# Stage 6 of a fused attention and expert kernel: second layer in three products of split operands

## The chip, the cores and the metric

The kernel runs on one core of a Trainium2 chip. Its engines have queues of their own: PE (TensorE, matmuls), DVE (VectorE), ACT (ScalarE), POOL (GpSimd) and SP (SyncE, which here issues DMAs). The metric is the time of one execution on the device in microseconds, lower is better.

## The reference

Three layers in a row over 1152 tokens (2 batches of 576), all in float32. The first is attention in which every query keeps its 32 largest scores; the second is a mixture of four experts, in which stage 6, the subject here, lies; the third is a feed-forward layer with the maximum of three products. In short:

```python
scores = scale * np.matmul(q, k.transpose(0, 1, 3, 2))
kth = np.partition(scores, -top_k, axis=-1)[..., -top_k:-top_k + 1]
attn = softmax(np.where(scores >= kth, scores, -1e9))     # 8 heads of 64
x = (attn @ v) as 1152 x 512
for e in range(4):                                         # _moe_ref
    h = np.maximum(x @ w1[e], 0.0)                         # 512 -> 1024
    out += p[:, e:e + 1] * (h @ w2[e])                     # 1024 -> 512
h = np.maximum(np.maximum(x @ w1, x @ w2), x @ w3)         # _moe2_ref, 512 -> 768
return h @ w_out
```

## The kernel before

The tokens are 9 tiles of 128. Attention goes tile by tile and pair of heads by pair of heads; its top-32 search (L443, L445) fills DVE for the first 440 us. PE has room meanwhile, and the kernel puts the experts' matmuls between those of attention. The experts run in stages that each take one, two or three tiles: `STAGES` is [0], [0,1], [1,2], [2,3], [3,4], [4,5], [5], [6,7,8], [6,7,8], counted from 0. A stage takes some of eight pieces `i` of the hidden layer: piece i is half of expert i // 2, and its two halves are u = 0, 1, 256 hidden units each. Stage 6 takes tile 5 alone (the sixth tile) with i = 0 to 3. Every (i, u) has a weight unit `a` of the first layer and one `b` of the second, 128x1024 each, keyed `(c, "a" or "b", i, u)` with c the stage.

**Two ways to multiply.** Most matmuls are done in three products (`product`, L680 to L682): each operand is split into a rounded high part (fp32r) and the low part that is left, and high x low, high x high and low x high are added up in PSUM. For a weight this takes a load to `raw` (L212), a copy by ACT to `whi` (L271) and a subtraction to `wlo` (L277), by POOL in two halves of 128x512 or, from a certain unit on (`LATE`), by DVE in one piece for every second unit. The hidden layer gets its high part from ACT with the relu and its low part from DVE (L822, L824); every `ON_POOL_H`-th time ACT writes `raw` (L815) and copies it (L816), and POOL subtracts (L817). The other way is a plain fp32 matmul of whole operands, slower per column but without splits. Stages in `WHOLE` (0 and 6) use it: in stage 6 `whole()` loads both `a` and `b` units straight into the buffers that hi and lo parts use elsewhere (L262 to L267), L801 does the first layer, ACT the relu (L804, `hfull`), and L842 the second layer, four matmuls of 128x512 for each i. A matmul in fp32 leaves two records in the trace, one in fp32r one.

**What sets the order.** One Python program writes out all instructions; engines then run their own queues strictly in that order. Attention's steps come first. Between them a planner adds expert work: `clock["dve"]` adds up a price for DVE work (`dve(n)`), `clock["goal"]` rises with it, and expert steps are put in until the priced PE work (`pe(n)`) reaches the goal. `later(...)` holds an evacuation back by one or two steps. `w_split_to` writes a weight's load and split `W_AHEAD` = 4 units before its use. There are five buffers each for raw, high and low parts. While the last stages of the experts run, the weights of the third layer, which come in a wide format, are converted in 48 pieces (`to_float32`: ACT L238 and L239, DVE L241 to L245, POOL L248 and a DMA on ACT's queue at L253); the first starts when attention is over. At about 582 us the first turned tiles (L900 transposes, ACT L906 and DVE L907 split) open the third layer.

**Names.** A tile's name carries a number that counts allocations, so the same tile has different numbers before and after. h_5640 is the last hidden block of stage 5, with its low part made by POOL; whi, wlo and raw are as above; psr (L517) are the transposed reciprocals of attention's row sums, ps1 and ps2 the sums of first and second layer, acc the gated sum of a tile (L743).

Of the kernel before, what the change touches and what calls it, by code (L numbers as in the profile page):

```python
# [10 lines left out]
F32 = mybir.dt.float32  # L11
# [3 lines left out]
AF = mybir.ActivationFunctionType  # L15
ALU = mybir.AluOpType
# [44 lines left out]
def kernel(  # L61
# [14 lines left out]
    nc = tc.nc  # L76
    B, HP, D, _, S = k.shape
    NT, DM = out.shape
    E = gates.shape[2]
    P = 128  # L80
# [20 lines left out]
    STAGES = [[0]] + [[t - 1, t] for t in range(1, NTILE - 3)] + [[NTILE - 4]] + [[NTILE - 3, NTILE - 2, NTILE - 1]] * 2  # L101
# [28 lines left out]
    def dve(n):  # L130
        clock["dve"] += 0.07 + n / 960.0

    def pe(n):
        clock["pe"] += n / 2400.0
# [63 lines left out]
    w_pos = {"load": 0, "split": 0}  # L198

    def whole(key):  # L200
        return key[1] in "ab" and key[0] in WHOLE

    def w_load_to(n):
        while w_pos["load"] < min(n, len(order)):
# [78 lines left out]
    def weight(key, oldest=None):  # L283

        w_split_to(w_index[oldest or key] + W_AHEAD + 2 * whole(key))
        return w_hl[key]
# [385 lines left out]
    def later(*stages):  # L672
        tick()
        lag.append(list(stages))
# [114 lines left out]
    def experts():  # L789
        begin = {}  # L790

        def half1(c, i, u):
            tiles = STAGES[c]
            N = len(tiles) * P
            if c in WHOLE:
                ps = bank("ps1")
                w = weight((c, "a", i, u)).rearrange("p (a f) -> p a f", f=256)
                for f in range(2):
                    for a in range(KT):
                        pe(4 * P)  # L800
                        nc.tensor.matmul(ps[:, f * P:(f + 1) * P], lhsT=w[:, a, f * P:(f + 1) * P], rhs=xfull[:, a, :], start=f == a == 0, stop=f == 1 and a == KT - 1)  # L801
                    yield True
                h = hp_.tile([P, 2, 512], F32, tag="h", bufs=4, name="hfull")[:, 0, 0:2 * P]
                later(lambda: [nc.scalar.activation(out=h, in_=ps[:, 0:2 * P], func=AF.Relu), made.add(("h", c, i, u))])  # L804
                yield h
                return
            for groups in layer1(weight((c, "a", i, u)), xs_of(tiles), N, begin.pop((c, i, u), None)):
                if groups is None:
                    tick()
                    yield True  # L810
            hh, hl = hidden(N)
            count = made_h[0] = made_h[0] + 1
            if ON_POOL_H and not count % ON_POOL_H:
                raw = ms.tile([P, 2 * WIDTH], F32, tag="tm", bufs=2, name="raw")
                later(lambda: [nc.scalar.activation(out=raw[:, g], in_=ps, func=AF.Relu) for g, ps in groups],  # L815
                      lambda: [nc.scalar.activation(out=hh[:, 0:2 * N], in_=raw[:, 0:2 * N], func=AF.Copy),  # L816
                               nc.gpsimd.tensor_tensor(out=hl[:, 0:2 * N], in0=raw[:, 0:2 * N], in1=hh[:, 0:2 * N].bitcast(F32), op=ALU.subtract),  # L817
                               made.add(("h", c, i, u))])
                yield hh, hl
                return  # L820
            dve(2 * N)
            later(lambda: [nc.scalar.activation(out=hh[:, g], in_=ps, func=AF.Relu) for g, ps in groups],  # L822
                  *[lambda: None] * H_LAG,
                  lambda: [nc.vector.scalar_tensor_tensor(out=hl[:, g], in0=ps, scalar=0.0, in1=hh[:, g].bitcast(F32),  # L824
                                                          op0=ALU.max, op1=ALU.subtract) for g, ps in groups]
                  + [made.add(("h", c, i, u))])
            yield hh, hl

        outs = {}

        def half2(c, i, hs, ti):
            t = STAGES[c][ti]
            if not i % 2:
                outs[t] = po.tile([P, DM], F32, tag="o", name="ps2") if ti < 2 else bank("ps2")
            ps = outs[t]
            assert {("h", c, i, 0), ("h", c, i, 1)} <= made
            if c in WHOLE:
                for u in range(2):
                    w = weight((c, "b", i, u), (c, "b", i, 0)).rearrange("p (f n) -> p f n", f=2)
                    for f in range(2):  # L840
                        pe(4 * DM)
                        nc.tensor.matmul(ps, lhsT=hs[u][:, f * P:(f + 1) * P], rhs=w[:, f, :], start=not i % 2 and u == f == 0, stop=i % 2 == 1 and u == f == 1)  # L842
                        yield True
            else:
                yield from layer2(ps, [weight((c, "b", i, u), (c, "b", i, 0)) for u in range(2)], hs, len(STAGES[c]) * P, ti, not i % 2, i % 2 == 1)
            if not i % 2:
                return
            first = t not in accs
            if first:
                sums(t)  # L850
            later(*[lambda: None] * E_LAG, gated(ps, t, i // 2, first, c == LAST_IN[t] and i == HALVES[c][-1]))

        before = None
        for c in range(1, len(STAGES)):
            phase[0] = c
            newest = max(STAGES[c])
            if c == 1:
                i = HALVES[c][0]
                for parts in (range(HP - 2), (HP - 2,)):
                    while (newest, parts[-1]) not in x_ready:  # L860
                        yield None
                    for n, x in enumerate([(i, 0), (i, 1), (i + 1, 0), (i + 1, 1)]):
                        if not parts[0]:
                            begin[(c, *x)] = (po if n < 2 else pg).tile([P, 512], F32, tag="go"[n < 2], name="ps1")
                        yield from begun(begin[(c, *x)], weight((c, "a", *x), (c, "a", i, 0)), xs_of(STAGES[c]), 2 * P, parts)
                        flush()
            while (newest, HP - 1) not in x_ready:
                yield None
            for i in HALVES[c]:
                hs = []  # L870
                for u in range(2):
                    for y in half1(c, i, u):
                        if y is not True:
                            hs.append(y)
                        yield True
                if i == HALVES[c][-1]:
                    x_free.update(t for t in STAGES[c] if LAST_IN[t] == c)
                if before is not None:
                    for ti in range(len(STAGES[before[0]])):
                        yield from half2(*before, ti)  # L880
                before = c, i, hs
        flush()
        yield from turned_ahead(len(STAGES))
        for ti in range(len(STAGES[before[0]])):
            yield from half2(*before, ti)
        flush()
# [193 lines left out]
```

## Time and profile before

| what | value |
|---|---|
| median of three runs | 749.8 us (749.56 to 750.65) |
| profiled execution, its own time | 748.98 us |
| its span on the core | 747.1 us |
| PE busy | 724.6 us, 97% |
| DVE, ACT, POOL busy | 605.4, 493.6, 459.4 us |
| granted PE clock | 1.0 over the whole span |
| L842 in stage 6 | 32 records of 0.592 us, from 429.9 to 465.1 us |

The span runs from the first to the last instruction; the rest of the execution's time lies around it. A row of the timeline begins with the start and the length in us; PE's rows overlap by the depth of its pipeline, so work is best read from the start of one group to the start of the next. An arrow in square brackets gives the idle time ahead of an instruction and what ended it.

### The profile page before, as it was taken

The page shows a single profiled execution, that of the slowest core. Times are in us where ns is not written, and L with a number is a line of the kernel's source. Part 1 is how long each engine was busy: PE and PEld are TensorE (multiplying, and loading weights), DVE is VectorE, ACT ScalarE, POOL GpSimd, SP SyncE. Part 2 cuts the span into 40 slices and gives each one's busy share as a digit, 9 for nine tenths or more (in the row PEclk, how much of TensorE's full clock was granted, in tenths as well). Part 3 has the DMA queues.
Part 4 walks back from the last instruction along what each step waited for, and adds up shares of the span by engine and source line. Part 5 has one row for each costly group of instructions (what it writes and reads, how often), then busy time and mean ns, then how long its engine had stood idle before and what let it go on. Part 6 is the DMA issues. An engine that isn't in the chain of part 4 may idle for free.

```text
span 747.1 us, 13552 instructions
## 1 busy us (share of the span) xinstructions
PE 724.6 (97%) x4678; PEld 641.4 (86%) x4678; DVE 605.4 (81%) x1160; ACT 493.6 (66%) x1127; POOL 459.4 (61%) x400
## 2 busy tenths in 40 slices
PE   6799999999999999999999999999999999999998
PEld 3587689888989989898988967999988899999996
DVE  6999989989999899999999958999999644233341
ACT  4668889899977787798796665666455533442531
POOL 2514778679979797698775216677676733442520
PEclk9999999999999999999999999999999999999999
DMA  7584555545647353545442859788788452443501
GB/s 220 180 269 160 147 174 175 156 127 159 194 123 209 108 195 122 154 126 162 144 121 91 288 182 363 240 268 278 231 259 255 157 191 76 154 170 99 196 2 43
DMA packets 56484, 130.14 MB, mean 174 GB/s; under 512 B 9760, under 2 KB 23328, under 8 KB 56416
## 3 DMA queue, kind: packets, MB, share of 16 engines
q1 hardware_dynamic: 48064, 120.69, 51.9%
q10 hardware_dynamic: 8352, 8.59, 3.2%
q8 instruction: 37, 0.61, 0.3%
q14 instruction: 31, 0.25, 0.1%
HBM read 120.60 MB, written 8.65 MB: 173 GB/s over the span
## 4 chain that ended last, share of the span: by engine, by line
PE 68%; DVE 13%; ACT 9%; POOL 4%; issue 3%; DMA 2%; ACTq 0%; POOLq 0%
PE ps L680 16%; PE ps L682 16%; PE ps L681 16%; DVE m L443 6%; DVE work L445 5%; POOL wlo L277 4%; PE psv L534 3%; ACT whi L271 3%; PE pss L423 2%; PE psp L489 2%; PE ps L842 2%; PE pso L680 2%; PE psa L765 2%; PE pso L681 2%; PE pso L682 2%
## 5 line engine op out<-in xcount | busy, mean ns | idle before, releaser
L277 POOL TENSOR_TENSOR wlo<-raw,whi 128x512 fp32r<-128x512 f32 x228 | 303.4, 1361 | 108.3 <-ACT whi L271 106.6
L271 ACT ACTIVATE whi<-raw 128x1024 fp32r<-128x1024 f32 x148 | 152.6, 1056 | 34.1 <-POOL narrow L248 14.6
L680 PE MATMUL ps<-xl,whi 128*128 128x256 f32 (+1 forms) x520 | 159.6, 307 | 0.6 <-POOL xl L555 0.6
L682 PE MATMUL ps<-xh,wlo 128*128 128x256 f32 (+1 forms) x520 | 156.5, 301 | 0.0
L681 PE MATMUL ps<-xh,whi 128*128 128x256 f32 (+1 forms) x520 | 156.4, 301 | 0.0
L443 DVE MAX8 m<-work 128x8 f32<-128x576 f32 x216 | 155.0, 743 | 0.1
L445 DVE MATCH_REPLACE8 work<-m,work 128x576 f32<-128x576 f32 x144 | 106.5, 740 | 0.0
L680 PEld LDWEIGHTS ps<-xl,whi 128*128 128x128 f32 x520 | 98.5, 189 | 1.9 <-POOL xl L555 0.8
L277 DVE TENSOR_TENSOR wlo<-raw,whi 128x1024 fp32r<-128x1024 f32 x34 | 53.5, 1573 | 56.4 <-ACT whi L271 45.2
L681 PEld LDWEIGHTS ps<-xh,whi 128*128 128x128 f32 x520 | 97.7, 188 | 1.2 <-issue 0.7
L682 PEld LDWEIGHTS ps<-xh,wlo 128*128 128x128 f32 x520 | 97.6, 188 | 0.0
L248 POOL TENSOR_TENSOR narrow<-narrow,raw 128x256 int32<-128x256 int32 x48 | 45.4, 947 | 40.0 <-DVE narrow L245 13.4
L680 PE MATMUL ps<-wlo,h 128*128 128x512 f32 x160 | 65.5, 410 | 0.6 <-POOL wlo L277 0.6
L682 PE MATMUL ps<-whi,h 128*128 128x512 f32 x160 | 62.8, 393 | 1.3 <-POOL h L817 1.3
L681 PE MATMUL ps<-whi,h 128*128 128x512 f32 x160 | 62.8, 392 | 0.0
L430 ACT ACTIVATE s<-pss 128x288 f32<-128x288 f32 x144 | 51.4, 401 | 11.8 <-PE pss L418 11.3
L443 DVE MAX8 m<-s 128x8 f32<-128x576 f32 x72 | 53.8, 747 | 3.9 <-ACT s L430 3.9
L445 DVE MATCH_REPLACE8 work<-m,s 128x576 f32<-128x576 f32 x72 | 53.3, 740 | 0.0
L682 PE MATMUL ps<-x2h,wlo 128*128 128x384 f32 x144 | 48.5, 336 | 0.0
L681 PE MATMUL ps<-x2h,whi 128*128 128x384 f32 x144 | 48.3, 335 | 0.0
L680 PE MATMUL ps<-x2l,whi 128*128 128x384 f32 x144 | 48.2, 335 | 0.0
L947 DVE TENSOR_TENSOR tm<-ps,tm 128x384 f32<-128x384 f32 x36 | 19.8, 554 | 33.6 <-PE ps L682 31.8
(118 smaller groups left out, 1616.2 us busy)
## 6 DMA issues: line engine op xcount, KB each, us to landing
raw<-in_w_dram SPq DMA_DIRECT2D x112, 512.0 KB, 4.2
raw<-narrow SPq DMA_DIRECT2D x36, 512.0 KB, 3.9
whole<-in_w_dram SPq DMA_DIRECT2D x30, 512.0 KB, 5.4
raw<-in_m_dram SPq DMA_DIRECT2D x36, 256.0 KB, 4.6
narrow<-narrow ACTq DMA_DIRECT2D x48, 128.0 KB, 4.7
kraw<-in_k_dram SPq DMA_DIRECT2D x16, 288.0 KB, 4.5
qraw<-in_q_dram SPq DMA_DIRECT2D x48, 64.0 KB, 3.9
raw<-in_mo_dram SPq DMA_DIRECT2D x12, 256.0 KB, 3.8
```

The costliest lines, as they stand in the source:

```text
L248: nc.gpsimd.tensor_tensor(out=out.bitcast(I32), in0=out.bitcast(I32), in1=last, op=ALU.add)
L271: nc.scalar.activation(out=hi, in_=raw, func=AF.Copy)
L277: on.tensor_tensor(out=lo[:, x], in0=raw[:, x], in1=hi[:, x].bitcast(F32), op=ALU.subtract)
L423: nc.tensor.matmul(ps[:, 0:SH], lhsT=l, rhs=r, start=i == 0, stop=i == len(mm) - 1)
L430: nc.scalar.activation(out=s[:, h, :], in_=halves[h][:, 0:SH], func=AF.Copy)
L443: nc.vector.max(m[:, 8 * r:8 * r + 8], src)
L445: nc.vector.match_replace(out=self.w[j], in_to_replace=m[:, 8 * r:8 * r + 8], in_values=src, imm_value=NEG)
L534: nc.tensor.matmul(ps[j * D:(j + 1) * D, cols], lhsT=vs[:, j * NR + r, :], rhs=self.pt[j][:, r, cols], start=False, stop=r == NR - 1)
L680: nc.tensor.matmul(ps, lhsT=lh, rhs=rl, start=first, stop=False)
L681: nc.tensor.matmul(ps, lhsT=lh, rhs=rh, start=False, stop=False)
L682: nc.tensor.matmul(ps, lhsT=ll, rhs=rh, start=False, stop=last)
L947: nc.vector.tensor_tensor(out=tm[:, g], in0=ps, in1=tm[:, g], op=ALU.max)
```

## The change

The second layer of stage 6 is done as everywhere else, in three products (`layer2`, L680 to L682), and no longer in fp32. So its eight `b` units are loaded to `raw` and split, and its hidden blocks get a high part (ACT with the relu, now L805) and a low part (DVE, now L806). The first layer of the stage stays in fp32. `dve(2 * P)` tells the planner of the new DVE work, which moves the places at which it puts expert work between attention's. What stood at L815 to L817 stands at L818 to L820 afterwards.

```diff
     def whole(key):
-        return key[1] in "ab" and key[0] in WHOLE
+        return key[1] == "a" and key[0] in WHOLE
...
-                h = hp_.tile([P, 2, 512], F32, tag="h", bufs=4, name="hfull")[:, 0, 0:2 * P]
-                later(lambda: [nc.scalar.activation(out=h, in_=ps[:, 0:2 * P], func=AF.Relu), made.add(("h", c, i, u))])
-                yield h
+                hh, hl = hidden(N)
+                dve(2 * P)
+                later(lambda: nc.scalar.activation(out=hh, in_=ps[:, 0:2 * P], func=AF.Relu),
+                      lambda: [nc.vector.scalar_tensor_tensor(out=hl, in0=ps[:, 0:2 * P], scalar=0.0, in1=hh.bitcast(F32), op0=ALU.max, op1=ALU.subtract),
+                               made.add(("h", c, i, u))])
+                yield hh, hl
...
-            if c in WHOLE:
-                for u in range(2):
-                    w = weight((c, "b", i, u), (c, "b", i, 0)).rearrange("p (f n) -> p f n", f=2)
-                    for f in range(2):
-                        pe(4 * DM)
-                        nc.tensor.matmul(ps, lhsT=hs[u][:, f * P:(f + 1) * P], rhs=w[:, f, :], start=not i % 2 and u == f == 0, stop=i % 2 == 1 and u == f == 1)
-                        yield True
-            else:
-                yield from layer2(ps, [weight((c, "b", i, u), (c, "b", i, 0)) for u in range(2)], hs, len(STAGES[c]) * P, ti, not i % 2, i % 2 == 1)
+            yield from layer2(ps, [weight((c, "b", i, u), (c, "b", i, 0)) for u in range(2)], hs, len(STAGES[c]) * P, ti, not i % 2, i % 2 == 1)
```

The first place is where stage 5 ends and stage 6 begins. On POOL before:

```order
L277 TENSOR_TENSOR wlo_5749<-raw_5539,whi_5748 128x512 x2
L277 TENSOR_TENSOR wlo_5754<-raw_5596,whi_5753 128x512 x2
L817 TENSOR_TENSOR h_5640<-raw_5641,h_5640 128x512
L555 TENSOR_TENSOR xl_121<-xt_5841,xh_120 128x128
L555 TENSOR_TENSOR xl_121<-xt_5983,xh_120 128x128
```

On POOL after:

```order
L277 TENSOR_TENSOR wlo_5749<-raw_5539,whi_5748 128x512 x2
L277 TENSOR_TENSOR wlo_5754<-raw_5596,whi_5753 128x512 x2
L277 TENSOR_TENSOR wlo_5819<-raw_5758,whi_5818 128x512 x2
L820 TENSOR_TENSOR h_5640<-raw_5641,h_5640 128x512
L555 TENSOR_TENSOR xl_121<-xt_5848,xh_120 128x128
L277 TENSOR_TENSOR wlo_5912<-raw_5762,whi_5911 128x512 x2
```

The split of the first `b` unit of stage 6 (wlo_5819) stands ahead of the low part of h_5640, and more such splits follow. On ACT at the same place, after:

```order
L818 ACTIVATE raw_5641<-ps1_5598 128x512
L271 ACTIVATE whi_5818<-raw_5758 128x1024
L519 ACTIVATE r_5804<-psr_5802 128x128
L819 ACTIVATE h_5640<-raw_5641 128x512
L805 ACTIVATE h_5815<-ps1_5747 128x256
```

The row of whi_5818 is new there; the other four stood in this order before.

The second place is the end of attention, in the middle of stage 6. h_6042 and h_6085 are the two hidden blocks of i = 2. On DVE before:

```order
L541 TENSOR_TENSOR xt_6111<-psv_6097,r_6109 128x128
L241 SCALAR_TENSOR_TENSOR raw64_6113<-narrow_6125,raw64_6113 128x256
L243 TENSOR_SCALAR narrow_6125<-raw64_6113 128x256
L245 SCALAR_TENSOR_TENSOR narrow_6125<-raw64_6113,narrow_6125 128x256
L241 SCALAR_TENSOR_TENSOR raw64_6115<-narrow_6141,raw64_6115 128x256
L243 TENSOR_SCALAR narrow_6141<-raw64_6115 128x256
L245 SCALAR_TENSOR_TENSOR narrow_6141<-raw64_6115,narrow_6141 128x256
L277 TENSOR_TENSOR wlo_6164<-raw_6062,whi_6163 128x1024
```

On DVE after:

```order
L541 TENSOR_TENSOR xt_6168<-psv_6154,r_6166 128x128
L241 SCALAR_TENSOR_TENSOR raw64_6170<-narrow_6182,raw64_6170 128x256
L243 TENSOR_SCALAR narrow_6182<-raw64_6170 128x256
L245 SCALAR_TENSOR_TENSOR narrow_6182<-raw64_6170,narrow_6182 128x256
L806 SCALAR_TENSOR_TENSOR h_6042<-ps1_6013,h_6042 128x256
L277 TENSOR_TENSOR wlo_6206<-raw_6051,whi_6205 128x1024
L806 SCALAR_TENSOR_TENSOR h_6085<-ps1_6045,h_6085 128x256
```

A weight split (wlo_6206, the last `b` unit of the stage) stands between the low parts of the two hidden blocks. ACT writes whi_6205, which it needs, as the third of three copies in a row behind the relu of h_6085:

```order
L805 ACTIVATE h_6085<-ps1_6045 128x256
L271 ACTIVATE whi_6191<-raw_6023 128x1024
L271 ACTIVATE whi_6198<-raw_6027 128x1024
L271 ACTIVATE whi_6205<-raw_6051 128x1024
L238 ACTIVATE narrow_6216<-raw64_6172 128x256
```

Before, only two weight copies stood between conversions there. On PE, which reads both low parts, before:

```order
L517 MATMUL psr_6107<-ident_87,rb_6092 128x128
L801 MATMUL ps1_6059<-xfull_122,whole_5922 128x128 x4
L842 MATMUL ps2_5975<-whole_5960,hfull_5957 128x512 x2
L842 MATMUL ps2_5975<-whole_5976,hfull_5973 128x512 x2
L801 MATMUL ps1_6157<-xfull_122,whole_6014 128x128 x8
L801 MATMUL ps1_6183<-xfull_122,whole_6016 128x128 x8
L842 MATMUL ps2_6207<-whole_6060,hfull_6057 128x512 x2
```

On PE after:

```order
L517 MATMUL psr_6164<-ident_87,rb_6149 128x128
L801 MATMUL ps1_6190<-xfull_122,whole_6021 128x128 x8
L801 MATMUL ps1_6226<-xfull_122,whole_6025 128x128 x8
L680 MATMUL ps2_6247<-wlo_6047,h_6042 128x512
L681 MATMUL ps2_6247<-whi_6046,h_6042 128x512
L682 MATMUL ps2_6247<-whi_6046,h_6042 128x512
L680 MATMUL ps2_6247<-wlo_6047,h_6042 128x512
L681 MATMUL ps2_6247<-whi_6046,h_6042 128x512
L682 MATMUL ps2_6247<-whi_6046,h_6042 128x512
L680 MATMUL ps2_6247<-wlo_6192,h_6085 128x512
L681 MATMUL ps2_6247<-whi_6191,h_6085 128x512
L682 MATMUL ps2_6247<-whi_6191,h_6085 128x512
```

More of stage 6 stands ahead of the last transposition psr than before, and the first matmul that reads the low part of h_6085 is the last row shown.

## Rows read from the trace of the kernel before

**Rows 1.** The page: busy time of the engines, and the granted clock in 40 slices.

```profile
PE 724.6 (97%) x4678; PEld 641.4 (86%) x4678; DVE 605.4 (81%) x1160; ACT 493.6 (66%) x1127; POOL 459.4 (61%) x400
...
PEclk9999999999999999999999999999999999999999
```

**Rows 2.** Busy time by stretch; the first number is its length, columns as in the header.

```profile
core 0: us, PE busy (x) PEld busy (x) DVE busy (x) ACT busy (x) POOL busy (x), PEclk, DMA share, GB/s
...
442.00:455.00 13.00, 13.00 (x72) 9.00 (x69) 9.64 (x17) 7.75 (x20) 6.82 (x7) 1.00 0.61 212
...
560.00:650.00 90.00, 90.00 (x481) 83.67 (x481) 50.79 (x73) 41.51 (x68) 45.33 (x35) 1.00 0.50 163
```

**Rows 3.** PE's waits from 405 to 455 us: total, times, longest.

```profile
PE psv L531 <- ACT pt L497: 1.2, 1, 1.2
```

**Rows 4.** Timeline of PE, end of stage 5: start, length, line, operation.

```profile
407.74 0.39 PE L680 MATMUL ps<-wlo,h 128*128 128x512 f32 x1
...
410.48 1.04 PE L489 MATMUL psp<-ident,p 128*128 128x128 f32 x8
...
417.14 0.48 PE L680 MATMUL ps<-wlo,h 128*128 128x512 f32 x1
...
418.62 0.29 PE L423 MATMUL pss<-kT,ql 128*128 128x288 f32 x1
...
419.62 0.39 PE L682 MATMUL ps<-whi,h 128*128 128x512 f32 x1
```

**Rows 5.** Timeline of PE, end of attention in stage 6.

```profile
442.32 0.33 PE L517 MATMUL psr<-ident,rb 128*128 128x128 f32 x1
...
443.38 3.60 PE L842 MATMUL ps<-whole,hfull 128*128 128x512 f32 x8
446.81 3.73 PE L801 MATMUL ps<-xfull,whole 128*128 128x128 f32 x32
450.38 3.60 PE L842 MATMUL ps<-whole,hfull 128*128 128x512 f32 x8
```

**Rows 6.** Timeline of ACT, the hidden block whose low part POOL makes.

```profile
415.48 0.59 ACT L815 ACTIVATE raw<-ps 128x512 f32<-128x512 f32 x1
415.95 0.28 ACT L519 ACTIVATE r<-psr 128x128 f32<-128x128 f32 x1
416.11 0.65 ACT L816 ACTIVATE h<-raw 128x512 fp32r<-128x512 f32 x1
```

**Rows 7.** Timeline of POOL, the same place.

```profile
409.58 5.02 POOL L277 TENSOR_TENSOR wlo<-raw,whi 128x512 fp32r<-128x512 f32 x4 [1.27 <-ACT whi L271]
...
416.83 1.29 POOL L817 TENSOR_TENSOR h<-raw,h 128x512 fp32r<-128x512 f32 x1 [2.24 <-ACT h L816]
```

**Rows 8.** DVE: one weight split in the timeline, and lines L277 and L824 (min/median/max ns).

```profile
448.13 2.00 DVE L277 TENSOR_TENSOR wlo<-raw,whi 128x1024 fp32r<-128x1024 f32 x1 [1.29 <-ACT whi L271]
...
L277 DVE TENSOR_TENSOR wlo<-raw,whi x34: 1210/1227/2378, 448.1 to 724.4; 128x1024 fp32r<-128x1024 f32 x34
...
L824 DVE SCALAR_TENSOR_TENSOR hl<-ps,hh x24: 540/545/550, 459.8 to 572.7; 128x384 fp32r<-128x384 f32 x24
```

**Rows 9.** Timeline of ACT behind the end of attention.

```profile
444.25 0.37 ACT L804 ACTIVATE hfull<-ps 128x256 f32<-128x256 f32 x1
...
446.10 1.05 ACT L271 ACTIVATE whi<-raw 128x1024 fp32r<-128x1024 f32 x1
...
447.05 1.05 ACT L271 ACTIVATE whi<-raw 128x1024 fp32r<-128x1024 f32 x1
```

**Rows 10.** Timelines of PE, POOL and DVE at the turn to the third layer.

```profile
584.87 0.40 PE L682 MATMUL ps<-whi,hl 128*128 128x512 f32 x1
591.29 0.34 PE L680 MATMUL ps<-x2l,whi 128*128 128x384 f32 x1
...
581.93 1.83 POOL L817 TENSOR_TENSOR hl<-raw,hh 128x768 fp32r<-128x768 f32 x1 [0.66 <-DMA narrow<-narrow]
...
589.75 1.41 DVE L907 TENSOR_TENSOR x2l<-pst,x2h 128x384 fp32r<-128x384 f32 x4
```

## Prediction

> **What bounds the kernel now.** I read the page first: TensorE is busy for 724.6 of 747.1 us, its clock is granted at full (2.4 GHz) in every slice, and no other engine is above 81% [rows 1]. The share is an average, so next come the stretches around stage 6 (the lone sixth tile) and behind it: from 442 us on PE is busy without a gap, 13.00 of 13.00 us and later 90.00 of 90.00, while DVE, ACT and POOL have room [rows 2]. The list of PE's waits between 405 and 455 us holds one entry, 1.2 us before the V product of the last attention pair [rows 3]; behind 455 us PE has no wait that the list shows. So from stage 6 on the time is PE's time: what PE no longer computes is gained, and any wait put into its row is lost in full, because the row keeps its order.
>
> The profiled execution took 748.98 us with a span of 747.1, so 1.9 us lie outside the span. It is 0.8 us below the median of 749.8. I make the sum as a difference and add it to the median.
>
> **Part 1, the matmuls.** Stage 6 has four second-layer blocks (i = 0 to 3). Before, each is four fp32 matmuls of 128x512, eight records, and from the start of one such block to the start of the next work is 446.81 - 443.38 = 3.43 us [rows 5]. After, each is twelve fp32r products; twelve such in a row took 410.48 - 407.74 = 2.74 us, 0.228 each [rows 4]. All four blocks now come behind fp32 work of layer 1; six products behind fp32 work took 418.62 - 417.14 = 1.48 instead of 6 x 0.228 = 1.37, so each change of type adds 0.11 [rows 4]. Four blocks: 4 x 3.43 = 13.72 becomes 4 x (2.74 + 0.11) = 11.40, a gain of 2.3 us. The bounds are 2.2 (0.03 more per block) and 2.8 (no cost of the change of type).
>
> The rows put twelve products at 0.80 of four fp32 matmuls. The Trainium skill (FP8 and Floating Point Precision, TensorE Precision Notes) counts true fp32 as four passes through the array; by that, three products would be 0.75 of it and the gain 3.4 us, which would take the sum below from +1.1 to 0.0. The rows differ from it by the change of type and by a spacing of 0.228 us, and I go by the rows.
>
> **Part 2, the eight extra splits.** The eight `b` weights of stage 6 used to land ready for use. Now each needs an ACT copy (whi), about 1.05 us, and a subtraction (wlo): on POOL in two halves, the run of four took 5.02 us or 1.255 each [rows 7], or for the last of the eight on DVE, 1.2 us median and up to 2.4 [rows 8]. That is 8.4 us of ACT and 17.6 us of POOL, under 40 us of PE, so the load fits; the bytes from memory are the same. What costs is place in a queue: ACT, POOL and DVE work strictly in the order shown under the change, and there are two places where a new split stands ahead of something that PE needs soon.
>
> *Stall 1, on POOL at about 420 us.* The last hidden block of stage 5 gets its low part from POOL (L817): before, ACT's copy starts at 416.11, POOL runs 416.83 to 418.12 [rows 6, 7], and PE first uses that low part in the L682 at 419.62 [rows 4], 1.5 us later. After, the new copy whi_5818 stands on ACT between the same block's L815 and L519, so it runs about 415.95 to 417.0. Its two halves stand on POOL directly ahead of the low part: 417.08 + 2 x 1.255 = 419.6, then the 1.29 us of the low part, ready at 420.9. PE's row up to there is the same in both kernels, so PE waits 420.9 - 419.62 = 1.3 us. This is the firmest term: 1.1 to 1.6. Behind the waiting L682 stand the scores of the next pair and the rest of layer 2.
>
> *Stall 2, on DVE just behind the end of attention.* Let T0 be the start of the last transposition of the row sums (L517), 442.32 before [rows 5]. After T0 PE now runs 16 layer-1 matmuls (32 records took 450.38 - 446.81 = 3.57 us; [rows 5] shows their start), six products (1.48) and two more (0.46), with 0.17 for the transposition itself: it wants the low part of h_6085 at T0 + 5.68. On ACT the relu of that block stands where L804 stood, at 444.25 or T0 + 1.93, followed by three copies 0.95 apart (446.10, 447.05 show the spacing) [rows 9], the third of which ends at about T0 + 5.15. On DVE the split wlo_6206 waits for that third copy, and the low part h_6085 stands behind it. The one such DVE split of that stretch, at 448.13, took 2.00 us while POOL was splitting too, the fastest 1.21 [rows 8]. The low part itself, 128x256, is about 0.4 us (128x384 took 0.54 [rows 8]). So it is ready at T0 + 5.15 + 1.21 + 0.4 = 6.75 or T0 + 5.15 + 2.0 + 0.4 = 7.5, and the stall is 1.1 to 1.8. POOL has two more halves running just then, as at 448 us, so I take 1.7.
>
> The row of 2.00 us beside 1.21 shows DVE held up while POOL works. The Trainium skill (SBUF — State Buffer, Who interferes with whom) says that DVE's second port pair is POOL's too, locked for a whole instruction. By that rule DVE would lose one POOL half of 1.26 us or two, and the sum below would come out at +1.4 or +2.6. By the row of 2.00 us I take a loss of 0.8.
>
> **Part 3, the relu's low parts.** Eight DVE operations of about 0.4 us are new, four of them ahead of the end of attention. Attention's chain goes through DVE, so T0 moves back by up to 1.6 us, and by stall 1. But the planner, which is told of that DVE time, also puts more PE work ahead of the last transposition (about 2 us), so PE is not idle for it. I take 0: the 1.2 us idle [rows 3] stays. Bounds: -1.2 (stall 1 uses up this idle, since PE then arrives later and its operand does not) and +1.6 (nothing covers the DVE work).
>
> **Part 4, later stages.** The eight splits use ACT and POOL in the place of conversions of the last layer's weights, which start when attention is over; these now run 2 to 4 us later relative to PE. With the load of 455 to 560 us this is hidden: PE has no waits there. At the turn to the last phase the cover is thin: the low part made by POOL from 581.93 for 1.83 us ends 1.1 us before PE's L682 at 584.87, and the last turned operand, from DVE's run of four at 589.75 for 1.41 us, should end by 591.16, just ahead of PE at 591.29 [rows 10]. There is less to convert ahead of each weight than before, too, so I take 0.2, with 0 and 2 as bounds.
>
> **The sum.** -2.3 + 1.3 + 1.7 + 0 + 0.2 = +0.9 us; with the rounding of the stalls, 0.7 to 1.3. That gives 749.8 + 0.9 = 750.7 us (profiled: about 749.9). A measurement of this kernel can tell about 0.2%, 1.5 us, from no change: 748.3 to 751.3 counts as same.
>
> **Rivals.**
> *Slower, because the late conversions reach the turn.* If the splits' 8.4 us on ACT and 17.6 on POOL are still partly owed at 582 us, the operands at 584.87 and 591.29 come late, by the lag of 2 to 4 us less a cover of 1.1 or 0.1. It decides from a lag of about 1.2 us left at 582. Price +1.5 to +3 us: 751.5 to 753.5. For it: POOL and ACT were already interleaved with conversions up to 580 us, and the cover there is the smallest of the row. Against it: PE ran without a wait through 455 to 650, and 2 to 3 fewer conversions stand ahead of the same weight. A double loss of the port at stall 2 (+1.26) leads to the lower end of it.
>
> *One stall only.* If stall 1 merely fills the 1.2 us that PE waits at 440.88 anyway, or stall 2 shrinks to its lower end and the port is free, the sum is -1.1 to +0.2: about 749.3. For: the wait of rows 3 lies between the two. Against: the last pair's exponentials wait for PE's scores, which stall 1 holds back as well.
>
> *No stall: the change brings just the matmuls.* The other engines' positions shift by as much as PE's, operands come in time, and the 2.3 us are gained: 747.5. For: shares of 55 to 80% on ACT and POOL in this stretch. Against: the order at both places, which timing does not change.
>
> **How the numbers follow.** Forecast (both stalls, nothing much at the turn) 0.43; slower rival 0.30; one stall 0.15; no stall 0.12. Faster by over 0.2% means below 748.3: all of no stall and little else, 0.13. Slower means above 751.3: most of the slower rival and the tail of the forecast, 0.33. Same: 0.54. The range goes from 748.4 (the one-stall case at its lower end) to 753.2; it leaves out the no-stall case and the far end of the slower rival.
>
> **What would show it.** Right: no L842 in stage 6 but 48 products in its place, at 0.228; a PE wait of 1.1 to 1.6 us on POOL's low part near 420; a PE wait of 1.1 to 1.8 us on DVE's low part about 6 us behind the last L517; no wait between 455 and 580; at 584 to 592 waits below 0.5 us. Wrong: the two waits missing or absorbed in the wait on the last pair, a wait on new weights (L680 on wlo) in stage 6, products slower than 0.228 us, or waits at the turn that add up to over 1 us.

## The result and the profile after

The changed kernel is slower: 754.7 us, median of six runs (752.54 to 755.06), against 749.6 for the kernel before (six runs, 749.32 to 750.65). The ratio is 1.0057, 95% interval 1.0045 to 1.0069. The range ended at 753.2. The profiled execution took 755.01 us with a span of 753.2; before it was 748.98 and 747.1.

The page and the stretches of after, as in [rows 1] and [rows 2]:

```profile
PE 724.9 (96%) x4694; PEld 644.7 (86%) x4694; DVE 616.0 (82%) x1169; ACT 501.4 (67%) x1135; POOL 479.9 (64%) x414
```

```profile
442.00:455.00 13.00, 10.67 (x85) 8.93 (x82) 5.67 (x12) 9.16 (x22) 5.36 (x5) 1.00 0.58 199
...
560.00:650.00 90.00, 87.89 (x455) 80.16 (x454) 58.92 (x84) 38.98 (x69) 47.01 (x38) 0.98 0.56 179
```

PE is no longer busy without a gap, and from 560 to 650 us its granted clock is below 1. PE's waits, first from 405 to 455 us and then from 560 to 650 us (total, times, longest); the kernel before has one in the first stretch [rows 3] and none in the second:

```profile
PE ps L682 <- DVE h L806: 1.5, 1, 1.5
PE ps L682 <- POOL h L820: 1.2, 1, 1.2
PE psv L531 <- ACT pt L497: 0.8, 1, 0.8
```

```profile
PE ps L682 <- POOL hl L820: 1.3, 1, 1.3
PE ps L680 <- ACT hh L819: 0.8, 1, 0.8
```

The same waits on PE's timeline (start, length, in brackets the wait and who ended it), with the two rows to which [rows 4] and [rows 10] answer:

```profile
421.90 0.50 PE L682 MATMUL ps<-whi,h 128*128 128x512 f32 x1 [1.15 <-POOL h L820]
...
454.56 0.50 PE L682 MATMUL ps<-whi,h 128*128 128x512 f32 x1 [1.53 <-DVE h L806]
...
587.40 0.51 PE L680 MATMUL ps<-wlo,hh 128*128 128x512 f32 x1 [0.81 <-ACT hh L819]
587.74 0.40 PE L681 MATMUL ps<-whi,hh 128*128 128x512 f32 x1
589.43 0.80 PE L682 MATMUL ps<-whi,hl 128*128 128x512 f32 x1 [1.29 <-POOL hl L820]
590.03 0.63 PE L680 MATMUL ps<-wlo,hh 128*128 128x512 f32 x1
590.45 0.63 PE L681 MATMUL ps<-whi,hh 128*128 128x512 f32 x1
...
597.36 0.34 PE L680 MATMUL ps<-x2l,whi 128*128 128x384 f32 x1
```

The two waits in stage 6 stand where the prediction put them, and have its size. What the forecast took as nearly nothing (0.2 us) is the turn to the third layer: the same instruction that started at 591.29 now starts at 597.36, 6.07 us later. **Where these 6.07 us came in**, read from the same instruction in both traces: 0.98 us stood already at 418 us; it came in by 332 us, ahead of the first instruction that the change moves, a load at 398 us (last section). The first stall brought it to 2.28 (421.90 against 419.62). When stage 7 is under way, where both rows run alike again, it is 1.07 (466.82 against 465.75): the matmuls have given back what the stalls took. By the transposes at the turn it is 2.03 (583.72 against 581.69), through two short waits for POOL's weight splits (468.37 and 542.84 us), each 0.45 us with the slower spacing behind it. From there to 597.36 it grows by 4.04: 2.1 us of waits, 0.4 of restarts (the wider spacing of products next to a wait), and seven products 0.35 to 0.60 us apart instead of 0.23, which is 1.5. In that stretch the granted clock is half (0.52):

```profile
589.43:592.51 3.08, 3.08 (x8) 2.47 (x8) 3.04 (x7) 2.76 (x7) 3.05 (x2) 0.52 0.96 363
```

To compare executions without what comes earlier, I count from a common point: the first product with the last hidden block of stage 5. The rows for before, then for after: that product, DVE's last operation of attention (L541), DVE's first turned low part (L907, after L902), PE's last matmul.

```profile
419.16 0.40 PE L680 MATMUL ps<-wlo,h 128*128 128x512 f32 x1
...
443.06 0.29 DVE L541 TENSOR_TENSOR xt<-psv,r 128x128 f32<-128x128 f32 x1 [3.72 <-ACT r L519]
...
583.01 0.75 DVE L907 TENSOR_TENSOR x2l<-pst,x2h 128x384 fp32r<-128x384 f32 x2 [1.13 <-ACT x2h L906]
...
743.19 0.40 PE L682 MATMUL pso<-whi,hl 128*128 128x512 f32 x1
```

```profile
420.12 0.40 PE L680 MATMUL ps<-wlo,h 128*128 128x512 f32 x1
...
447.96 0.29 DVE L541 TENSOR_TENSOR xt<-psv,r 128x128 f32<-128x128 f32 x1 [4.01 <-ACT r L519]
...
589.59 0.74 DVE L902 TENSOR_TENSOR x2l<-pst,x2h 128x384 fp32r<-128x384 f32 x2
...
749.26 0.40 PE L682 MATMUL pso<-whi,hl 128*128 128x512 f32 x1
```

**A** is the time from that product to attention's end, **S** the stretch from there to the first turned low part, in which the conversions stand, **T** the whole to the last matmul's end. Before: A = 443.35 - 419.16 = 24.2, S = 139.7, T = 324.4. After: A = 28.1, S = 141.3, T = 329.5. So 5.1 us belong to the change: attention ends 3.9 later, the stretch behind it is 1.7 longer, and the rest is 0.5 shorter. The same numbers from every run's trace, with the conversions that stand on DVE in S:

| kernel | median, us | ratio to before, 95% | A | S | T | conversions in S |
|---|---|---|---|---|---|---|
| before | 749.1 to 750.0 |  | 24.2 | 139.7 | 324.4 | 47 |
| after | 754.7 | 1.0057 (1.0045 to 1.0069) | 28.1 | 141.3 | 329.5 | 45 |
| e1_no_stall1 | 753.0 | 1.0055 (1.0038 to 1.0071) | 26.7 | 141.3 | 328.3 | 45 |
| e2_no_stall2 | 754.9 | 1.0078 (1.0063 to 1.0093) | 28.1 | 141.3 | 329.7 | 45 |
| e3_no_stalls | 752.9 | 1.0052 (1.0034 to 1.0071) | 26.7 | 141.3 | 328.3 | 45 |
| e4_turn_dve | 753.8 | 1.0062 (1.0046 to 1.0078) | 28.1 | 139.2 | 329.5 | 44 |
| f1_low_on_act | 753.4 | 1.0048 (1.0030 to 1.0065) | 28.2 | 141.4 | 328.2 | 45 |
| f2_no_charge | 752.6 | 1.0030 (1.0016 to 1.0043) | 25.8 | 141.1 | 327.2 | 46 |
| f3_before_dve_ops | 750.4 | 1.0006 (0.9993 to 1.0018) | 24.2 | 139.9 | 324.5 | 47 |
| f4_matmuls_alone | 749.9 | 0.9994 (0.9982 to 1.0005) | 24.1 | 139.7 | 324.2 | 47 |
| s1_splits_alone | 755.7 | 1.0084 (1.0072 to 1.0097) | 26.3 | 143.5 | 330.2 | 47 |
| k1_fewer_before_turn | 750.5 | 1.0009 (1.0001 to 1.0018) | 28.1 | 135.8 | 325.1 | 40 |
| k2_all_mended | 749.3 | 0.9998 (0.9989 to 1.0006) | 24.8 | 138.2 | 324.1 | 41 |
| k3_before_fewer | 749.1 | 0.9994 (0.9985 to 1.0004) | 24.2 | 139.7 | 324.4 | 43 |
| b1_mended_later_conv | 747.1 | 0.9969 (0.9960 to 0.9979) | 24.8 | 136.7 | 322.0 | 41 |
| b2_mended_fewer | 754.6 | 1.0068 (1.0055 to 1.0082) | 24.7 | 136.7 | 329.2 | 37 |
| h1_late_half | 754.2 | 1.0067 (1.0052 to 1.0081) | 24.9 | 144.2 | 329.7 | 46 |

The medians were taken in groups beside runs of before, which stood at 749.6 for after, 749.1 for e, 750.0 for f, 749.5 for k and h, and 749.3 for s and b. T is free of that, but it comes from one execution each: those of after and of e1 to e4 hold about 1.5 us of half clock at the turn, b2 and h1 have half clock in other places, and the rest have none between 405 us and the last microseconds.

### The profile page after: what moved, and what is told of

Read it like the earlier page. It is cut to its first block, busy times and chain, and to the rows that moved or that the text cites. A ratio compares the mean times of both kernels' runs of the same rounds, so it can differ in the third digit from the quotient of the medians.

```text
span 753.2 us, 13623 instructions
## 1 busy us (share of the span) xinstructions
PE 724.9 (96%) x4694; PEld 644.7 (86%) x4694; DVE 616.0 (82%) x1169; ACT 501.4 (67%) x1135; POOL 479.9 (64%) x414
## 4 chain that ended last, share of the span: by engine, by line
PE 45%; DVE 28%; ACT 13%; issue 5%; DMA 5%; POOL 4%; ACTq 0%; SPq 0%; POOLq 0%; DVEq 0%
DVE m L443 11%; PE ps L682 10%; PE ps L680 10%; PE ps L681 9%; DVE work L445 8%; ACT whi L271 4%; DMA raw<-in_w_dram 3%; POOL wlo L277 2%; PE psv L534 2%; PE psa L765 2%; PE pso L680 2%; PE pso L681 2%; PE pso L682 2%; DVE raw L241 1%; DVE narrow L243 1%
## 5 line engine op out<-in xcount | busy, mean ns | idle before, releaser
L277 POOL TENSOR_TENSOR wlo<-raw,whi 128x512 fp32r<-128x512 f32 x242 | 322.3, 1360 | 117.0 <-ACT whi L271 115.4
L271 ACT ACTIVATE whi<-raw 128x1024 fp32r<-128x1024 f32 x156 | 161.1, 1056 | 40.5 <-POOL narrow L248 14.5
L680 PE MATMUL ps<-xl,whi 128*128 128x256 f32 (+1 forms) x520 | 158.9, 305 | 0.4 <-POOL xl L555 0.4
L682 PE MATMUL ps<-xh,wlo 128*128 128x256 f32 (+1 forms) x520 | 156.6, 301 | 0.1
L680 PEld LDWEIGHTS ps<-xl,whi 128*128 128x128 f32 x520 | 98.5, 189 | 1.4 <-POOL xl L555 0.6
L682 PEld LDWEIGHTS ps<-xh,wlo 128*128 128x128 f32 x520 | 97.6, 188 | 0.5 <-POOL wlo L277 0.5
L277 DVE TENSOR_TENSOR wlo<-raw,whi 128x1024 fp32r<-128x1024 f32 x35 | 53.7, 1534 | 52.4 <-ACT whi L271 41.3
L682 PE MATMUL ps<-whi,h 128*128 128x512 f32 x176 | 69.3, 394 | 4.0 <-POOL h L820 2.4
L680 PE MATMUL ps<-wlo,h 128*128 128x512 f32 x176 | 72.1, 410 | 0.6 <-POOL wlo L277 0.6
L248 POOL TENSOR_TENSOR narrow<-narrow,raw 128x256 int32<-128x256 int32 x48 | 47.8, 997 | 35.4 <-DVE narrow L245 12.7
L681 PE MATMUL ps<-whi,h 128*128 128x512 f32 x176 | 69.0, 392 | 0.0
L682 PE MATMUL ps<-x2h,wlo 128*128 128x384 f32 x144 | 48.5, 336 | 0.0
L680 PE MATMUL ps<-x2l,whi 128*128 128x384 f32 x144 | 48.2, 335 | 0.0
L942 DVE TENSOR_TENSOR tm<-ps,tm 128x384 f32<-128x384 f32 x36 | 19.6, 554 | 31.4 <-PE ps L682 29.6
```

The lines of the kernel that those rows point to most:

```text
L248: nc.gpsimd.tensor_tensor(out=out.bitcast(I32), in0=out.bitcast(I32), in1=last, op=ALU.add)
L271: nc.scalar.activation(out=hi, in_=raw, func=AF.Copy)
L277: on.tensor_tensor(out=lo[:, x], in0=raw[:, x], in1=hi[:, x].bitcast(F32), op=ALU.subtract)
L680: nc.tensor.matmul(ps, lhsT=lh, rhs=rl, start=first, stop=False)
L681: nc.tensor.matmul(ps, lhsT=lh, rhs=rh, start=False, stop=False)
L682: nc.tensor.matmul(ps, lhsT=ll, rhs=rh, start=False, stop=last)
```

## The experiments

**The two stalls, taken away by order.**

```diff
# e1: in w_split_to
-            if w_pos["load"] == w_pos["split"]:
+            if w_pos["load"] == w_pos["split"] or key == (6, "b", 0, 0) and ("h", 5, HALVES[5][-1], 1) not in made:
                 return
# e2: low = the scalar_tensor_tensor of L806, relu = the activation of L805
+                later(*([lambda: [relu(), low()]] if (c, i, u) == (6, 2, 1) else [relu, low]))
```

> The changed kernel, but the split of the first second-layer weight of stage 6 is put behind the low part of the last hidden block of stage 5 on POOL (and its copy one pair later on ACT); everything else keeps its order. Both theories: the PE wait of 1.2 us on POOL's low part near 420 us goes. Theory L (the lag of the conversions sets the turn to the third layer, at 584 to 592 us): attention and the conversions that follow it come 1.2 us earlier as well, so all of it is gained, about 753.4 us against 754.7, and the waits at the turn stay at about 2.1 us. Theory S (each stall adds its own length): the same 753.4. Rival: the wait on the last pair's V product grows by what is saved and nothing is gained: 754.7.

> The changed kernel, but DVE makes the low part of the hidden block of i = 2, u = 1 of stage 6 ahead of the last weight split of the stage instead of behind it; the other engines keep their order. Both theories: the PE wait of 1.5 us near 453 us goes. Theory S: all of it is gained, about 753.1 us. Theory L: PE comes 1.5 us earlier to the turn, where it waits for the hidden block's high and low part that the conversions hold back; the two waits there grow from 2.1 to about 3.6 us and the time stays at 754.4 to 754.9.

> Both edits of the two kernels before. Theory S: 754.7 - 1.2 - 1.6 = 751.9 us with waits of 2.1 us at the turn. Theory L: as without the first stall alone, about 753.4 us, with waits of about 3.6 us at the turn.

Measured: 753.0, 754.9 and 752.9 us. The first stall gave back 1.2 us of T: PE waited there while attention's scores stood behind it, and A fell from 28.1 to 26.7. The second gave back nothing, alone or with the first. In the place of its 1.5 us PE waits 0.9 us on POOL's split of stage 7's first weight and a few tenths more in the products behind it; at the transposes of the turn PE stands where it stood in after, 163.6 us behind the common point in both, and there the block's two waits are 0.8 and 1.3 us as ever:

```profile
PE ps L682 <- POOL h L820: 1.1, 1, 1.1
PE ps L682 <- POOL wlo L277: 0.9, 1, 0.9
PE psv L531 <- ACT pt L497: 0.8, 1, 0.8
```

(PE's waits of e2 from 400 to 500 us.) So a PE wait behind attention's end does not add to the time here; one ahead of it does. That is what theory L said of the time. Its mechanism was off: the waits at the turn did not grow to 3.6 us, for PE waited for late weight splits from stage 7's first weight on.

**The turn's hidden block by DVE.**

```diff
-            if ON_POOL_H and not count % ON_POOL_H:
+            if ON_POOL_H and not count % ON_POOL_H and (c, i, u) != (8, 3, 1):
```

> The changed kernel, but the last hidden block of stage 8 gets its high part from ACT with the relu and its low part from DVE, instead of by ACT's raw copy, ACT's second copy and POOL; both stand one conversion earlier in ACT's and DVE's order. The waits on that block at the turn (0.8 and 1.3 us) should go, and with them the stretch at half clock that follows them (about 1.5 us). If the lag bears on that block alone: 754.7 - 4.0 = 750.7 us. If it bears on all operands of the turn, a wait on the turned tiles' low part or on the third layer's first weights takes its place at about 597 us: 752 to 753.5 us.

Measured: 753.8 us, just above the range, T unchanged at 329.5. Both waits on the block went, and a wait of 1.8 us on the turned tiles' low part took their place (profile of e4, PE's waits from 575 to 640 us), with half clock behind it from 596.4 to 599.8 us (0.51). The lag is not that block's; it bears on the turned tiles too.

```profile
PE ps L680 <- DVE x2l L902: 1.8, 1, 1.8
```

**Whose work makes the lag.** Five kernels that each take or add one part (edits shortened):

```diff
# f1: the low part's place goes to ACT, as zeros
+                      lambda: [nc.scalar.activation(out=hl, in_=ps[:, 0:2 * P], func=AF.Copy, scale=0.0),
# f2
-                dve(2 * P)
# f3: before, behind the relu's stage
+ lambda: nc.vector.scalar_tensor_tensor(out=extra, in0=ps[:, 0:2 * P], scalar=0.0, in1=h, op0=ALU.max, op1=ALU.subtract)   # i >= 2
# f4: before, L842
-                        nc.tensor.matmul(ps, lhsT=hs[u][:, f * P:(f + 1) * P], rhs=w[:, f, :], ...)
+                        product(ps.rearrange("p (s n) -> p s n", s=2), [hs[u][:, f * P:(f + 1) * P]] * 2, [stand_in] * 2, ...)
# s1: before, whole() without stage 6's b units; L842 reads the high part as f32
+                    w = weight((c, "b", i, u), (c, "b", i, 0))[0].bitcast(F32)
```

> The changed kernel, but the eight low parts of stage 6 (DVE, 0.41 us each) are written by ACT as zeros at the same places of the program; it leaves out the subtraction that makes the low part. Theory D (DVE's row sets the time as far as the turn to the third layer: attention up to its end, and then the conversions, 141.3 us from the end of attention to the first turned low part): attention's end comes 4 x 0.41 = 1.6 us earlier and the stretch behind it is 1.6 us shorter, so about 3.3 us are gained, 751.4 us against 754.7, and the stretch measures 139.7 us again. Theory P (PE's row sets it, DVE's load counts only where PE waits on it): the 1.5 us stall on the low part near 453 us goes, 753.2 us, and the stretch has no say.

> The changed kernel without dve(2 * P): the planner isn't told of the new DVE work and puts twelve products and four first-layer matmuls that stood ahead of attention's last transposition behind it. Theory D: attention ends 1 to 3 us earlier, the conversions start as much earlier, and the time falls by about that: 752 to 753.7 us. Theory P: PE's work is only moved, and the stalls on POOL's and DVE's low parts stay: 754 to 755 us.

> The kernel before, with four DVE operations of 128x256 (0.41 us each) added behind the end of attention, on the places of the low parts of i = 2 and 3; nobody reads what they write, and every other engine's row is that of before. Theory D: the stretch from attention's end to the first turned low part grows from 139.7 to 141.3 us, and PE, which came to the turned operands 0.1 us after they were ready, now waits about 1.6 us there: 749.6 + 1.6 = 751.2 us, up to 752.8 with half clock behind the wait. Theory P: 749.6 us, PE has no wait on DVE.

> The kernel before, with each of the sixteen fp32 matmuls of the second layer of stage 6 replaced by three fp32r products of the same size, on unsplit stand-ins (the relu's output on both sides; the second layer's weights land but aren't used, so the result of this tile is left out). Other engines and the planner's order are as before. PE's row gets about 2.3 us shorter. Theory P: all of it is gained, 747.3 us. Theory D: attention's end and the conversions stay where they are, PE waits about 2 us for operands at the turn: 748.9 to 749.6 us, and no less than 749.6 if the wait brings half clock with it.

> The kernel before, with the eight second-layer weights of stage 6 loaded and split as in the changed kernel, while the second layer stays in fp32 and reads the high part alone (the low part of these weights is left out of the result) and the relu stays whole. PE's row is that of before, no low parts, no planner's charge. If the splits are what costs: attention's end comes 1.4 us later (the first split stands ahead of the low part on POOL), the stretch from there to the first turned low part is 141.3 us instead of 139.7, and the time is 749.6 + 3.1 = 752.7 us, up to 754 with half clock at the turn. If the low parts and the planner's order are the larger share: 750.8 to 751.2 us.

f4 is the plainest: the matmuls alone, about 2.3 us less for PE and no other engine's order touched, gained nothing that can be measured (749.9 us against 750.0). Counted from the common point, PE came to the transposes of the turn 2.2 us earlier than before and to the first turned operand only 0.4 earlier. Most of the difference is a wait of 1.2 us for POOL's low part, the one whose lead of 1.1 us [rows 10] shows for before:

```profile
585.25 0.50 PE L682 MATMUL ps<-whi,hl 128*128 128x512 f32 x1 [1.17 <-POOL hl L817]
```

f3 and f1 refute theory D as I had put it. Four more DVE operations in the stretch cost nothing that can be measured (S 139.9), and moving the eight low parts to ACT left A and S as they were; the 1.3 us of T that f1 gained lie at the turn, where its waits are 1.4 us instead of 2.1 and no half clock follows. Half clock alone is 1.5 us, and after too has executions without it, so a gain by the edit itself is not shown. f1 does not show that the low parts cost nothing ahead of attention's end, since ACT had the eight operations instead. In f2 the first step of the expectation came true: without the charge the twelve products stand behind the last transposition, and A falls by 2.3 to 25.8. But of the 2.4 us that T falls, 1.5 are the half clock, which follows the two waits of the turn (0.8 and 1.2 us here) in after's profile and not in f2's. At the transposes of the turn f2 is 0.9 us ahead of after (162.7 against 163.6 from the common point). That its median meets theory D's range may in part be luck. s1 tells what the splits do: alone they cost 6.4 us (755.7 against 749.3), twice what I had expected, with A at 26.3 (the first stall, and a wait for the last pair that grew from 1.2 to 1.9) and S at 143.5. In S the conversions themselves got slower, as the sum of DVE's records there shows: the 47 last steps of a conversion (L245) took 27.8 us before and 30.3 in s1, the 47 first steps (L241) 31.4 and 32.5. Over S, DVE is busy for 129.2 of 139.7 us in before and 133.7 of 141.3 in after, nearly full but not full; PE is busy for all of S in before and for 137.4 of 141.3 in after:

```profile
443.35:583.01 139.66, 139.66 (x707) 123.33 (x706) 129.21 (x190) 84.31 (x173) 98.90 (x83) 1.00 0.82 263
```

```profile
448.25:589.59 141.34, 137.40 (x708) 123.52 (x706) 133.66 (x190) 86.78 (x174) 106.27 (x86) 1.00 0.78 243
```

So in before S is the length of PE's row, with the conversions close behind it. In s1, where PE has the same work as in before, S grows by 3.8 us: there the conversions and splits set it.

**The stretch relieved.**

```diff
# k1: after; k3: the same in the kernel before; k2: with e1, e2 and f2; the price of a conversion for the planner (its three steps alike)
-        dve(1024 // WIDE)
+        dve(1.4 * 1024 // WIDE)
# b1: k2 and
-WIDE, W_FROM, W_STEP = 4, 306, 2
+WIDE, W_FROM, W_STEP = 4, 308, 2
```

> The changed kernel with only the planner's price of a conversion raised by 1.4, so that 40 instead of 45 conversions stand on DVE between the end of attention and the turn to the third layer, and five come later, where DVE is busy a third of the time. Theory C (the chain of conversions between attention's end and the turn sets the time; PE waits for it): that stretch gets shorter than 141 us by several us, PE comes through without waits at the turn, and what is left is PE's row with the two stalls: 754.7 - 4 = 750.7 us. Theory P (attention's end 4 us later is the loss, however many conversions stand behind it): 754 to 755 us. Rival: the five late conversions hold back weights of the third layer and the wait only moves to later than 600 us.

> The kernel before with the price of a conversion raised by 1.4 and nothing else (43 instead of 47 conversions ahead of the turn). Its PE had no wait at the turn, so theory C expects no gain: 749.4 to 749.9 us. If it comes out at 747 to 748.5 us, the gain of the kernel with all edits isn't that of the matmuls.

> The changed kernel without the two stalls of stage 6 (both edits of the no-stalls kernel), without the planner's charge for the low parts, and with the price of a conversion raised by 1.4 (41 conversions ahead of the turn). Theory C: PE's row alone is left, with 2.3 us less in it: 749.8 - 2.3 = 747.3 us, 746.8 to 748.3. If a wait comes in another place: 749 to 751 us.

> The kernel with all edits (no first stall, low part of i = 2, u = 1 with its relu, no planner's charge, price of a conversion 1.4), and the first conversion one step later, so that the low part of i = 2, u = 0 stands ahead of it on DVE and ACT. PE waited 1.2 us on that low part; if that goes: 749.3 - 1.2 = 748.1 us, below both kernels. If the later conversions come late for the turn instead: 749.3 us.

k1 changes nothing in stage 6, keeps both stalls and attention's late end (A 28.1), and takes five conversions out of the stretch. The time falls to 750.5 us, T to 325.1, 0.7 above before. The turn's waits shrink to one of 0.3 us. It is close to the 0.7 that the prediction's sum gives without its last term, but the parts differ: k1 stands only 0.1 us behind before at the transposes of the turn, and the rest comes in at the turn itself. k3 shows that the edit is worth nothing by itself, 749.1 against 749.5: with 43 conversions DVE is busy for only 118.1 us of S, and S is 139.7 us as in before, since PE's row sets it. k2 missed its 747.3: T 324.1, because without the charge another low part (i = 2, u = 0) stands behind the first conversion on DVE and PE waits 1.2 us on it. b1 takes that away, and all that PE still waits for from 405 us to the end is the last pair:

```profile
PE psv L531 <- ACT pt L497: 1.5, 1, 1.5
```

b1 takes 747.06 us (746.68 to 748.81) against 749.29. That beats both kernels by more than the measurement is uncertain. Its gain, 2.2 us (2.4 of T), fits the 2.3 us of the matmuls, and it stands where they are: at the transposes of the turn b1 is already 2.4 us ahead of before (160.1 against 162.5 from the common point), and it keeps that to the end. No run moves the first conversion in the kernel before, but there the only wait of PE that this could shorten is the 1.2 us of [rows 3], and in b1 that wait is longer.

Two runs show the limits of it.

> As the kernel of the run before, with the price of a conversion raised by 1.8 instead of 1.4, so that fewer stand ahead of the turn. If the 0.3 us that PE still waited for the turned tiles' low part comes from the conversions: 747.8 us. If the late ones hold back the third layer's weights: over 749 us.

> Half of the change: only the blocks i = 2 and 3 of stage 6, whose splits and low parts stand mostly behind the end of attention, are done in three products; i = 0 and 1 stay in fp32, so no split stands ahead of the last hidden block of stage 5 and attention's row on PE is nearly that of before. Theory C: attention ends within 1 us of before (counted from stage 5's last product), the stretch behind it is 141 us instead of 139.7 for the extra splits, and PE waits at the turn: 750.5 to 752 us, up to 1.5 us more with half clock. Theory P: two blocks' worth of PE time is gained less the stall on DVE's low part, 749.8 - 1.15 + 1.5 = 750.1 us without a wait at the turn.

With 1.8 times the price (b2, 37 conversions ahead of the turn) a split of the third layer's last weights came late, one wait of 4.5 us and half clock behind it: 754.6 us. h1, only blocks i = 2 and 3 in three products, was a miss: 754.2 instead of 750.5 to 752. There the low part of i = 2, u = 1 stands on DVE behind a split and a whole conversion, PE waits 4.1 us on it, and the clock falls to half (windows of h1):

```profile
450.00:455.00 5.00, 2.14 (x11) 1.41 (x9) 4.93 (x6) 2.18 (x5) 5.00 (x4) 0.97 0.79 205
455.00:460.00 5.00, 3.75 (x10) 3.37 (x11) 4.93 (x9) 3.41 (x7) 4.26 (x4) 0.50 0.87 308
```

## Why the prediction was wrong, step by step

- **The bound.** "So from stage 6 on the time is PE's time" is the step that failed. It was read from PE having no wait. That says who is last, not by how much: the operands of the turn were ready only 0.1 and 1.1 us ahead of PE, and [rows 10] had both numbers. f4 shows that the bound was shared: about 2.3 us off PE alone gain nothing that can be measured.
- **Part 1, the matmuls.** Right in size. Twelve products took 466.64 - 463.91 = 2.73 us, and b1 got 2.2 us for them once nothing else was in the way. Not all four blocks stand behind fp32 work, as the text has it: this one follows fp32r products. The gain of 3.4 us, which the prediction works out from four passes for fp32 in the Trainium skill (FP8 and Floating Point Precision, TensorE Precision Notes), did not show. The +1.1 and 0.0 beside it don't belong to the sum below: from its +0.9 that gain would lead to -0.2.
- **Part 2, the stalls.** Right in place and size: 1.3 against 1.3 (1.15 of wait and the restart), 1.5 against 1.7. The weight split ahead of the second took 1.76 us, between the two bounds; that is 0.55 over the fastest one, less than one POOL half of 1.26 us. The first cost its length because it also holds back attention (e1); the second cost nothing in this kernel (e2).
- **Part 3, attention's end.** I let it move freely as long as PE had work. PE did have it, and A grew by 3.9: 1.4 by the first stall (e1), 2.3 by the work that the planner puts ahead (f2). Each of these moves the start of the conversions. The turn moved with it by 1.4 us in e1, and by 0.9 in f2. The term of PE's own wait, taken as 0, measured -0.4: 0.8 instead of 1.2 us ahead of the V product.
- **Part 4, the later stages.** The term that was mis-sized by it: 0.2, bounds 0 to 2. It measured 5.0: 1.0 in two short waits up to the turn and 4.0 at it. I had the lag (2 to 4 us) and the leads there, and then set them off against "fewer conversions ahead"; two fewer did not make up for the splits (S + 1.7, and + 3.8 for the splits alone in s1).
- **The rivals.** What happened is the first rival, with a chance of 0.30. Its price, 1.5 to 3, was too low, because it took the wait alone and left out the half clock behind it, 1.5 us in the profiled execution. That the port at stall 2 would be lost twice the runs did not bear out, and whether the four low parts ahead of attention's end cost something no run settles.

What stays open: which of ACT, POOL and DVE sets the pace of the conversions and splits. DVE is the busiest of the three in S (133.7 of 141.3 us in after, ACT 86.8, POOL 106.3), and POOL's grew most (98.9 to 106.3), but no run takes POOL's splits away alone. That added DVE work in before was free (f3) doesn't clear DVE: it was idle for 10 us of S there.

## What to carry to other kernels

An engine that is busy without a gap can be one of several bounds; before costing a change on it, look for the operand that reaches it with the smallest lead, and treat that chain as a second bound with its own start and its own work. A wait that a change adds costs its length where it holds back the start of that chain, and nothing where the chain is awaited later anyway, as e1 and e2 show for this kernel. Work that a planner prices can be moved off a full stretch by its price alone, and k1, b1 and b2 show that there is too little and too much of it.

## What the runs showed of the hardware

**Half clock behind a short wait.** Behind waits of 0.8 and 1.3 us, with 0.7 us of work between them, PE's granted clock is half, 1.2 instead of 2.4 GHz (0.52 from 589.43 to 592.51), and the spacing of products is 0.43 instead of 0.23 us (590.03, 590.45 above). Of the six runs of after, the four that took 754.5 us or more show a mean clock of 0.997 or 0.998, the two at 752.54 and 753.77 one of 1.0. So one program shows both outcomes. In f2 waits of 0.8 and 1.2 us stand at the same place, and its clock stays at 1.0 in the profile. A single wait was followed by half clock in e4 (1.8 us), not in f1 (1.4) and b1 (1.5). What decides it the runs don't show.

**A microsecond by chance.** The 0.98 us ahead of the first moved instruction come mostly from one DVE operation, in the same order in both kernels. Before, then after:

```profile
330.20 1.14 DVE L471 SCALAR_TENSOR_TENSOR p<-s,m,p 128x576 f32<-128x576 f32 x1
...
330.67 1.27 POOL L367 TENSOR_TENSOR ql<-qraw,qh 128x256 fp32r<-128x256 f32 x1
```

```profile
330.47 1.86 DVE L471 SCALAR_TENSOR_TENSOR p<-s,m,p 128x576 f32<-128x576 f32 x1
...
330.94 0.78 POOL L367 TENSOR_TENSOR ql<-qraw,qh 128x256 fp32r<-128x256 f32 x1
```

Where the DVE operation takes 1.14 us, POOL's takes 1.27; where it takes 1.86, POOL's takes 0.78. Elsewhere the same DVE operation takes 0.80 us (415.74 in before). DVE's is longer than that in both rows and POOL's in one, and how much each loses differs between two executions with the same order up to there. The Trainium skill (SBUF — State Buffer, Who interferes with whom) describes a port pair shared by the two engines and held for a whole instruction by the one that issues first, with the other blocked. The trace agrees in part: in after one engine loses and the other doesn't (POOL 0.78, DVE 1.86 us), but DVE's row starts first, by 0.47 us, in both traces, and in before neither has its shorter length (1.27 and 1.14 us). It makes 0.7 us of difference between these two executions.
